# Loading V from ScalarE's hardware queue instead of SyncE's in a one-token attention kernel

## The chip, the core and the metric

The kernel runs on one core of a Trainium2 chip. The metric is the device time of one execution in microseconds (us). Before the change the median of three runs is 1298.89 us (1298.85 to 1299.34).

The core has five instruction streams: TensorE (PE, with its weight loads as PEld), VectorE (DVE), ScalarE (ACT), GpSimd (POOL) and SyncE (SP). All transfers between main memory and on-chip memory are moved by the core's 16 DMA engines, whichever stream issues them. A stream issues its own instructions in order; streams wait for one another only on semaphores.

## The reference, cut to what matters

```python
def _A_ref(x, k_cache, v_cache, wq, wo):        # x: (2, 1, 512); caches: (2, 32, 8192, 128), float32
    B, Sq, D = x.shape
    H, Dh = 32, 128
    q = (x @ wq).reshape(B, Sq, H, Dh).transpose(0, 2, 1, 3)
    scores = jnp.einsum("bhqd,bhkd->bhqk", q, k_cache) * (Dh ** -0.5)
    p = _softmax(scores, axis=-1)
    o = jnp.einsum("bhqk,bhkd->bhqd", p, v_cache)
    return o.transpose(0, 2, 1, 3).reshape(B, Sq, H * Dh) @ wo
...
x = A_x
xn = _layernorm(x, axis=-1)
s = _A_ref(xn, A_k_cache, A_v_cache, A_wq, A_wo)
g = _silu(_B_ref(xn, B_w1, B_b1, B_w2, B_b2))   # a small MLP of each token
return x + s * g
```

Two tokens, 32 heads each, 8192 cached keys and values of 128 floats per head. The caches of K and V are 268 MB each, and every number of them is used once.

## The kernel before, in words

**Tiling.** The 64 (token, head) combinations are taken two at a time: `N = 32` pairs, numbered n = 0 to 31. K of a pair is 8 MB and is laid out on 128 partitions with 64 KB on each (a head has 64 partitions, a partition has 128 keys). V of a pair has the same layout. One load of K or V is thus one DMA of 128 rows of 64 KB, 8 rows for each of the 16 DMA engines.

**Buffers.** K has two buffers, `kb[0]` and `kb[1]`, used in turn. V has a single buffer, `vb`, which at the start also holds the weights of the small parts and at the end the matrix `wo`. V of the last pair goes to `kb[1]` instead.

**The work on a pair n.** VectorE multiplies K by the query in place in two halves (`scores_mul`, L559), adds up each key's products in two halves (`scores_sum`, L566) and takes the largest score (`max_rows`, L570). PE and VectorE turn this into the largest score of each head (`max_dve`, L573 and L576). ScalarE computes the exponentials into `PZ` (`exps`, L583 to L591). PE multiplies them with V in 32 matmuls (`weighted`, L610, 64 matmul records in the profile), ScalarE copies the result out of the accumulator (`O4`, L617), PE picks each head's part (L619) and VectorE stores it into `Z` (`spread`, L625).

**The order on VectorE.** The steps of two neighbouring pairs are interleaved by hand. In turn n VectorE runs: first half of the product for pair n, the head's maximum for pair n-1, second half of the product, both sums for pair n, the maximum, and `spread` of pair n-1. So `weighted(n-1)` needs the exponentials of pair n-1, which come after the first product of pair n; and the last step of VectorE's turn n needs `weighted(n-1)`.

**The order on SyncE's queue.** All loads are issued by SyncE, in program order: ..., V(n), K(n+2), V(n+1), K(n+3), ... V(n) waits until `weighted(n-1)` has read `vb`. K(n+2) waits until `scores_sum(n)` has read its buffer. At the end come V(31) in two halves, and `wo` in seven pieces, which wait until `weighted(30)` has read `vb`.

**Loops.** A planner (`Plan`) collects all operations, derives the semaphore waits from what each reads and writes, and puts the operations that repeat from pair to pair into a hardware loop of its own on each engine. SyncE has no loop: its loads are written out one by one. ScalarE's loop runs over turns 1 to 31 and holds `exps` and the copy of `O4`.

Of the kernel before, what the change touches and what calls it, by code (L numbers as in the profile page):

```python
# [21 lines left out]
class Plan:  # L22
# [18 lines left out]
    def op(self, eng, fn, r=(), w=(), over=(), it=None, loop=False, dma=None):  # L41


        o = Op()
        o.eng, o.fn, o.it, o.loop, o.dma, o.tell = eng, fn, it, loop, dma, False
        need = {}

        def after(d, war):
            if d.dma is None and dma is None and d.eng == eng and (eng == "pe" or war):
                return  # L50
            if d.dma is None:
                if need.get(d.eng) is None or need[d.eng].idx < d.idx:
                    need[d.eng] = d
            else:
                k = ("dma", d.dma)
                if need.get(k) is None or need[k].idx < d.idx:
                    need[k] = d

        for k in r:
            if k in self.writer:  # L60
                after(self.writer[k], False)
        for k in list(w) + list(over):
            if k in self.writer:
                after(self.writer[k], False)
            for d in self.readers.get(k, ()):
                after(d, True)
        clock = self.clock[eng]
        need = {k: d for k, d in need.items() if clock.get(k, 0) < d.idx}
        o.deps = [(k, d) for k, d in need.items()
                  if not any(e is not d and e.done.get(k, 0) >= d.idx for e in need.values())]  # L70
        for _, d in o.deps:
            for k, v in d.done.items():
                clock[k] = max(clock.get(k, 0), v)
        own = eng if dma is None else ("dma", dma)
        self.count[own] = o.idx = self.count.get(own, 0) + 1
        o.done = dict(clock)
        o.done[own] = o.idx
        for k in w:
            self.writer[k] = o
            self.readers[k] = []  # L80
        for k in r:
            if k not in w:
                self.readers.setdefault(k, []).append(o)
        self.ops.append(o)
# [80 lines left out]
def decode_kernel(nc, x, kc, vc, wq, wo, w1, b1, w2, b2, out):  # L165
    P = 128
    B, H, S, DH = kc.shape
# [3 lines left out]
    U = 2  # L171
    HP = P // U
    KP = S // HP
    HH = H // U
    N = B * HH
# [25 lines left out]
    op = plan.op  # L201

    def pe(fn, r=(), w=(), it=None, loop=False):
        op("pe", fn, r, w, it=it, loop=loop)
# [4 lines left out]
    def act(fn, r=(), w=(), it=None, loop=False):  # L209
        op("act", fn, r, w, it=it, loop=loop)  # L210
# [4 lines left out]
    def sbuf(name, shape):  # L215
        return nc.alloc_sbuf_tensor(name, shape, F32).ap()

    def psum(name, shape):
        return nc.alloc_psum_tensor(name, shape, F32).ap()
# [5 lines left out]
    vb = sbuf("vb", [P, KP * DH])  # L225
    kbuf = [t.rearrange("p (j d) -> p j d", d=DH) for t in kb]
    vbuf = vb.rearrange("p (j d) -> p j d", d=DH)
# [19 lines left out]
    half = sbuf("half", [P, UP])  # L247
# [6 lines left out]
    ZR = sbuf("ZR", [P, B * P])  # L254

    PZ = sbuf("PZ", [P, NT, U, JW])
# [4 lines left out]
    BIAS = sbuf("bias", [P, U])  # L261
    RS = sbuf("rs", [P, 1])
    O4 = sbuf("o4", [P, JW * DH])
# [9 lines left out]
    boot = []  # L273

    def take(name, p, n, base=0, at=None):

        if at is None:
            at = used[0]
            used[0] += n
            assert used[0] <= KP * DH  # L280
        boot.append(name)
        return vb[base:base + p, at:at + n]
# [22 lines left out]
    h = take("h", P, WR * B).rearrange("p (r b) -> p r b", b=B)  # L305
# [5 lines left out]
    PO = psum("po", [P, JW * DH])  # L311
# [6 lines left out]
    def bank():  # L318
        i = turn[0] % 4
        turn[0] += 1  # L320
        return scratch[i], f"s{i}"
# [3 lines left out]
    vf = vc.rearrange("b h s d -> (b h s d)").rearrange("(n p j d) -> n p j d", p=P, j=KP, d=DH)  # L325
    M = KP // 2

    def load(dst, src, sem, w, over=()):
        op("sp", lambda: nc.sync.dma_start(dst, src), (), w, over=over, dma=sem)  # L329

    def load_k(n):
        i = (n + 1) % 2
        if n in (0, N - 1):
            for s in range(2):
                load(kbuf[i][:, s * M:(s + 1) * M], kf[n][:, s * M:(s + 1) * M], f"k{i}{s}", [("kb", i, s)])
            return
        load(kbuf[i], kf[n], f"kb{i}", [("kb", i, s) for s in range(2)])
# [186 lines left out]
    for k in range(N // NB):  # L524

        b, e = divmod(k, HH // NB)
        i, g = divmod(e, GQ)
        p, kp = bank()
# [9 lines left out]
    PT, PM, PN = (t for t in scratch[:3])  # L538
    load_k(1)

    def load_v(n):
        load(vbuf, vf[n], "v", ["vb"], over=boot)

    def cols(t, a, n):

        return t[:, a:a + n] if isinstance(a, int) else t[:, bass.ds(a, n)]
# [32 lines left out]

    def exps(n):  # L580
        one = dict(it=n + 1, loop=n < N - 1)
        pe(lambda i: matmul(PN[:, :U], srow, NM, start=True, stop=True), ["srow", "nm"], ["s2"], **one)  # L582
        act(lambda i: nc.scalar.copy(BIAS, PN[:, :U]), ["s2"], ["bias"], **one)  # L583
        sc = SC.rearrange("p (t j) -> p t j", j=JW)
        for s in range(U):
            r = slice(HP * s, HP * (s + 1))
            act(lambda i, r=r, s=s: nc.scalar.activation(PZ[r, :, s, :], sc[r], AF.Exp, bias=BIAS[r, s:s + 1],  # L587
                                                         scale=SCALE, accum_out=RS[r]),
                ["bias", ("sc", 0), ("sc", 1)], [("PZ", s), ("rs", s)], **one)

        act(lambda i: nc.scalar.activation(cols(ZR, i * UP - UP, UP), half, AF.Copy, scale=RS),  # L591
            ["half"] + [("rs", s) for s in range(U)], [("ZR", n)], **one)

    def busy(n):

        for _ in range(n):
            pe(lambda: matmul(scratch[3], ident, Q[:, :512], start=True, stop=True),
               ["ident"] + [("Q", k) for k in range(512 // (NB * DH))], ["s3"])

    def weighted(n):  # L600

        one = dict(it=n + 1, loop=n < N - 1)
        last = n == N - 1
        v = kbuf[1] if last else vbuf
        for t in range(NT):
            j = t % QT
            keys = [("kb", 1, t * JW // M)] if last else ["vb"]
            pe(lambda i, t=t, j=j, v=v: matmul(PO[R * j:R * j + U * JW, :], PZ[:, t].rearrange("p s j -> p (s j)"),  # L610
                                               v[:, t * JW:(t + 1) * JW, :].rearrange("p j d -> p (j d)"),
                                               start=(t < QT), stop=(t + QT >= NT)),
               keys + [("PZ", s) for s in range(U)], ["po"], **one)
        if last:
            busy(1)

        act(lambda i: nc.scalar.copy(O4, PO), ["po"], ["o4"], **one)  # L617
        for k in range(JW):
            pe(lambda i, k=k: matmul(PT[:, :U], O4[:, k * DH:(k + 1) * DH], mod[:, k:U * JW:JW],  # L619
                                     start=(k == 0), stop=(k == JW - 1)), ["o4", "mod"], ["s0"], **one)  # L620
# [9 lines left out]
    for n in range(N):  # L630
        scores_mul(n, 0)
        if n:
            max_dve(n - 1)
            exps(n - 1)
        scores_mul(n, 1)
        if n == 0:
            gates()
            load_v(0)

        if n:  # L640
            weighted(n - 1)
            if n < N - 1:
                load_v(n)
        scores_sum(n, 0)
        scores_sum(n, 1)
        max_rows(n)
        if n:
            spread(n - 1)

        if n + 2 < N:  # L650
            load_k(n + 2)
        elif n + 2 == N:
            for s in range(2):
                load(kbuf[1][:, s * M:(s + 1) * M], vf[N - 1][:, s * M:(s + 1) * M], f"v1{s}", [("kb", 1, s)])
# [7 lines left out]

    max_dve(N - 1)
    exps(N - 1)
    weighted(N - 1)
    spread(N - 1)

# [91 lines left out]
```

## Time and profile before

| | |
|---|---|
| median of three runs | 1298.89 us |
| profiled execution, its own time | 1298.97 us |
| its span (first to last instruction) | 1297.7 us |
| bytes read from main memory | 559.30 MB |
| mean rate over the span | 431 GB/s |
| ScalarE busy | 78.0 us (6%) |
| PE busy | 411.7 us (32%) |

The profile of one execution is read in several views. One lists the engines' busy time; one lists the DMA queues with packets, megabytes and the share of the 16 DMA engines' time that their packets took; one (the chain of waits) follows the last instruction back, at each step to what released it; one lists groups of equal instructions with count, total busy time and mean nanoseconds of one; the timeline lists instructions in order: start, duration, engine, line, operation, output<-input, count, and in brackets how long the engine stood idle before it and what released it. "SPq" is the issuing of a DMA by SyncE. "Windows" gives busy time in a chosen stretch.

### The profile page before, as it was taken

The page shows a single profiled execution, that of the slowest core. Times are in us where ns is not written, and L with a number is a line of the kernel's source. Part 1 is how long each engine was busy: PE and PEld are TensorE (multiplying, and loading weights), DVE is VectorE, ACT ScalarE, POOL GpSimd, SP SyncE. Part 2 cuts the span into 40 slices and gives each one's busy share as a digit, 9 for nine tenths or more (in the row PEclk, how much of TensorE's full clock was granted, in tenths as well). Part 3 has the DMA queues.
Part 4 walks back from the last instruction along what each step waited for, and adds up shares of the span by engine and source line. Part 5 has one row for each costly group of instructions (what it writes and reads, how often), then busy time and mean ns, then how long its engine had stood idle before and what let it go on. Part 6 is the DMA issues. An engine that isn't in the chain of part 4 may idle for free.

```text
span 1297.7 us, 6944 instructions
## 1 busy us (share of the span) xinstructions
PE 411.7 (32%) x2796; PEld 123.9 (10%) x2796; DVE 1138.0 (88%) x294; ACT 78.0 (6%) x250; POOL 1.4 (0%) x8
## 2 busy tenths in 40 slices
PE   5602333312333312333311333321333321333327
PEld 1100011000101000101100101000001100001103
DVE  3699999888889988889988889988888988888991
ACT  1200000000000000000000000000000000000000
POOL 0000000000000000000000000000000000000000
PEclk9856666556666556666555666655666655666659
DMA  9999999999999999999999999999999999999998
GB/s 400 449 425 440 428 428 442 426 442 426 434 438 424 446 424 440 430 426 444 426 438 430 428 442 426 442 426 432 440 424 446 424 440 430 424 446 426 427 430 373
DMA packets 11231, 559.42 MB, mean 431 GB/s; under 512 B 1364, under 2 KB 1620, under 8 KB 1880
## 3 DMA queue, kind: packets, MB, share of 16 engines
q1 hardware_dynamic: 11224, 559.33, 99.7%
q8 instruction: 4, 0.07, 0.0%
q14 instruction: 3, 0.02, 0.0%
HBM read 559.30 MB, written 0.03 MB: 431 GB/s over the span
## 4 chain that ended last, share of the span: by engine, by line
DMA 72%; PE 23%; DVE 3%; issue 1%; ACT 0%; SPq 0%; another core or an unknown queue 0%; DVEq 0%; ACTq 0%
DMA vb<-in_A_v_cache_dram 67%; PE po L610 22%; DMA kb<-in_A_wq_dram 3%; DMA vb<-in_A_wo_dram 2%; DVE kb L559 1%; DVE sc L566 1%; PE po L518 1%; SPq L329 0%; PE acc L703 0%; PE s L531 0%; PE wide L711 0%; ACT PZ L587 0%; DVE gate L503 0%; PE s L582 0%; ACT Q L533 0%
## 5 line engine op out<-in xcount | busy, mean ns | idle before, releaser
L559 DVE TENSOR_TENSOR kb<-kb,Q 128x8192 f32<-128x8192 f32 x64 | 555.6, 8682 | 107.9 <-DMA kb<-in_A_k_cache_dram 96.7
L566 DVE TENSOR_REDUCE sc<-kb 128x64 f32<-128x8192 f32 x64 | 552.3, 8666 | 0.0
L610 PE MATMUL po<-vb,PZ 128*8 128x512 f32 x1984 | 288.8, 748 | 293.7 <-DMA vb<-in_A_v_cache_dram 292.0
L582 PE MATMUL s<-nm,srow 1*128 1x2 f32 x64 | 18.4, 355 | 364.1 <-DVE nm L576 364.1
L610 PEld LDWEIGHTS po<-vb,PZ 128*8 128x8 f32 x1984 | 57.5, 104 | 499.0 <-issue 497.2
L573 PE MATMUL s<-ident,mx 128*1 128x128 f32 x32 | 11.8, 369 | 180.2 <-DVE mx L570 180.2
L582 PEld LDWEIGHTS s<-nm,srow 1*128 1x128 f32 x64 | 15.7, 302 | 373.3 <-DVE nm L576 373.3
L617 ACT COPY o<-po 128x512 f32<-128x512 f32 x32 | 18.8, 586 | 541.7 <-PE po L610 541.7
L583 ACT COPY bias<-s 128x2 f32<-128x2 f32 x32 | 5.1, 160 | 609.3 <-PE s L582 609.3
L619 PE MATMUL s<-mod,o 128*128 128x2 f32 x256 | 33.6, 253 | 22.1 <-ACT o L617 22.1
L619 PEld LDWEIGHTS s<-mod,o 128*128 128x128 f32 x256 | 31.1, 191 | 51.3 <-ACT o L617 51.3
L587 ACT ACTIVATE PZ<-sc,bias 64x128 f32<-64x128 f32 x64 | 25.5, 399 | 1.8
L573 PEld LDWEIGHTS s<-ident,mx 128*1 128x1 f32 x32 | 2.5, 79 | 183.0 <-DVE mx L570 183.0
L625 DVE TENSOR_TENSOR Z<-blk,s 128x8 f32 (+1 forms) x32 | 5.2, 163 | 12.4 <-PE s L619 12.4
L443 DVE COPY vb<-vb 2x384 f32<-2x384 f32 x4 | 1.8, 500 | 14.7 <-ACT vb L439 14.7
L587 ACT ACTIVATION_READ_ACCUMULATOR PZ<-sc,bias 64x1 f32 x64 | 11.8, 185 | 0.0
L435 PE MATMUL s<-vb 128*2 128x512 f32 (+1 forms) x24 | 11.3, 620 | 0.3 <-ACT vb L393 0.3
L570 DVE TENSOR_REDUCE mx<-sc 128x1 f32<-128x128 f32 x32 | 9.1, 286 | 1.1
L591 ACT ACTIVATE ZR<-half,rs 128x8 f32 (+1 forms) x32 | 9.6, 301 | 4.1
L518 PE MATMUL po<-kb,vb 128*4 128x512 f32 x64 | 8.4, 684 | 2.6 <-DMA kb<-in_A_wq_dram 2.6
L610 PE MATMUL po<-kb,PZ 128*8 128x512 f32 x64 | 8.8, 709 | 1.4 <-ACT PZ L587 1.4
L576 DVE TENSOR_REDUCE nm<-s 1x2 f32<-1x128 f32 x32 | 8.7, 272 | 0.3 <-PE s L573 0.3
(101 smaller groups left out, 80.7 us busy)
## 6 DMA issues: line engine op xcount, KB each, us to landing
kb<-in_A_k_cache_dram SPq DMA_DIRECT2D x4, 4096.0 KB, 43.3
kb<-in_A_v_cache_dram SPq DMA_DIRECT2D x2, 4096.0 KB, 40.4
vb<-in_B_w_dram SPq DMA_DIRECT2D x2, 2752.0 KB, 12.3
vb<-in_A_wo_dram SPq DMA_DIRECT2D x1, 4096.0 KB, 19.8
vb<-in_A_wo_dram SPq DMA_DIRECT2D x1, 2048.0 KB, 24.3
vb<-in_A_wo_dram SPq DMA_DIRECT2D x1, 1280.0 KB, 26.9
vb<-in_A_wo_dram SPq DMA_DIRECT2D x2, 256.0 KB, 27.0
vb<-in_A_v_cache_dram SPq DMA_DIRECT2D x31, 29.2
```

What stands on the lines that cost most here:

```text
L435: pe(lambda f=f, w=w, ph=ph, c=c: matmul(ph[:B, :w], yT[:, c, :], w1_sb[:, c, f:f + w], start=(c == 0), stop=False), ["yT", "w1"], [k])
L518: pe(lambda i=i, c=c, wv=wv, a=a, j=j, hd=hd: matmul(PO[R * j:R * j + NQ * B, :].rearrange("m (h d) -> m h d", d=DH), xnT[:, c, a:a + NQ * ...
L559: vector(n, n, lambda n: nc.vector.tensor_tensor(out=k, in0=k, in1=cols(Q, n * DH, DH).unsqueeze(1).to_broadcast([P, M, DH]), op=ALU.mult) ...
L566: vector(n, n, lambda n: nc.vector.tensor_reduce(out=SC[:, s * M:(s + 1) * M], in_=k, axis=AX.X, op=ALU.add), [("kb", i, s)], [("sc", s)])
L570: vector(n, n, lambda n: nc.vector.tensor_reduce(out=MX, in_=SC, axis=AX.X, op=ALU.max), [("sc", 0), ("sc", 1)], ["mx"])
L573: pe(lambda i: transpose(PM[:1, :P], MX, ident), ["mx", "ident"], ["s1"], it=n, loop=n > 0)
L582: pe(lambda i: matmul(PN[:, :U], srow, NM, start=True, stop=True), ["srow", "nm"], ["s2"], **one)
L587: act(lambda i, r=r, s=s: nc.scalar.activation(PZ[r, :, s, :], sc[r], AF.Exp, bias=BIAS[r, s:s + 1], scale=SCALE, accum_out=RS[r]), ["bias ...
L591: act(lambda i: nc.scalar.activation(cols(ZR, i * UP - UP, UP), half, AF.Copy, scale=RS), ["half"] + [("rs", s) for s in range(U)], [("ZR" ...
L610: pe(lambda i, t=t, j=j, v=v: matmul(PO[R * j:R * j + U * JW, :], PZ[:, t].rearrange("p s j -> p (s j)"), v[:, t * JW:(t + 1) * JW, :].rea ...
L617: act(lambda i: nc.scalar.copy(O4, PO), ["po"], ["o4"], **one)
L619: pe(lambda i, k=k: matmul(PT[:, :U], O4[:, k * DH:(k + 1) * DH], mod[:, k:U * JW:JW], start=(k == 0), stop=(k == JW - 1)), ["o4", "mod"], ...
```

## The change

V of pairs 1 to 30 is issued by ScalarE inside its loop, right behind the copy of `O4`. V(0) stays with SyncE, as does V(31). The buffers, the arithmetic and the waits for the buffers stay as they were. For the address of V(n) the loop's register is used. ScalarE's loop runs over turns 1 to 30 instead of 1 to 31; the last turn is written out behind it (`two`, and the copy of `O4`, with `loop=n < N - 2`).

```diff
+    vrows = vc.rearrange("b h s d -> (b h s d)").rearrange("(n p e) -> n p e", p=P, e=KP * DH)
+
     def load_v(n):
-        load(vbuf, vf[n], "v", ["vb"], over=boot)
+        if n == 0:
+            load(vbuf, vf[0], "v", ["vb"], over=boot)
+            return
+        op("act", lambda i: nc.scalar.dma_start(
+            vb, vrows[i if isinstance(i, int) else bass.ds(i, 1)].rearrange("p e -> p e" if isinstance(i, int) else "o p e -> (o p) e")),
+            (), ["vb"], it=n, loop=n < N - 1, dma="v")
...
     def exps(n):
         one = dict(it=n + 1, loop=n < N - 1)
+        two = dict(it=n + 1, loop=n < N - 2)
...
-        act(lambda i: nc.scalar.copy(O4, PO), ["po"], ["o4"], **one)
+        act(lambda i: nc.scalar.copy(O4, PO), ["po"], ["o4"], it=n + 1, loop=n < N - 2)
```

SyncE's queue at the first pairs, before (`kb0`, `kb1` and `vb` are the buffers; each row is one DMA):

```order
L329 DMA kb1<-in_A_k_cache_dram 128x8192 x2
L329 DMA kb0<-in_A_k_cache_dram 128x16384
L329 DMA vb<-in_A_v_cache_dram 128x16384
L329 DMA kb1<-in_A_k_cache_dram 128x16384
L329 DMA vb<-in_A_v_cache_dram 128x16384
L329 DMA kb0<-in_A_k_cache_dram 128x16384
L329 DMA vb<-in_A_v_cache_dram 128x16384
```

The same place, with the change:

```order
L329 DMA kb1<-in_A_k_cache_dram 128x8192 x2
L329 DMA kb0<-in_A_k_cache_dram 128x16384
L329 DMA vb<-in_A_v_cache_dram 128x16384
L329 DMA kb1<-in_A_k_cache_dram 128x16384
L329 DMA kb0<-in_A_k_cache_dram 128x16384
L329 DMA kb1<-in_A_k_cache_dram 128x16384
```

The 30 rows of V between the rows of K are gone; a load of K now follows the load of K before it, and no load of V stands between.

ScalarE's loop before, from its first row to the branch back:

```order
L583 COPY bias<-s 128x2
L107 ISA
L587 ACTIVATE PZ,rs<-sc,bias 64x32x4 x2
L107 REGISTER_ALU
L591 ISA
L591 ACTIVATE ZR<-half,rs 128x8
L107 REGISTER_ALU
L617 COPY o<-po 128x512
L158 REGISTER_ALU
L158 COMPARE_AND_BRANCH
```

The same loop with the change (line numbers are 8 higher in the new file):

```order
L591 COPY bias<-s 128x2
L107 ISA
L595 ACTIVATE PZ,rs<-sc,bias 64x32x4 x2
L107 REGISTER_ALU
L599 ISA
L599 ACTIVATE ZR<-half,rs 128x8
L107 REGISTER_ALU
L625 COPY o<-po 128x512
L547 ISA
L547 DMA vb<-in_A_v_cache_dram 128x16384
L158 REGISTER_ALU
L158 COMPARE_AND_BRANCH
```

The load stands at the end of the turn, behind the copy that already waits for the last matmul on `vb`.

More of the change, by code (lines that the diff above doesn't have):

```diff
@@ L581, in exps @@
         one = dict(it=n + 1, loop=n < N - 1)
+        two = dict(it=n + 1, loop=n < N - 2)
         pe(lambda i: matmul(PN[:, :U], srow, NM, start=True, stop=True), ["srow", "nm"], ["s2"], **one)
-        act(lambda i: nc.scalar.copy(BIAS, PN[:, :U]), ["s2"], ["bias"], **one)
+        act(lambda i: nc.scalar.copy(BIAS, PN[:, :U]), ["s2"], ["bias"], **two)
         sc = SC.rearrange("p (t j) -> p t j", j=JW)
@@ L588, in exps @@
                                                          scale=SCALE, accum_out=RS[r]),
-                ["bias", ("sc", 0), ("sc", 1)], [("PZ", s), ("rs", s)], **one)
+                ["bias", ("sc", 0), ("sc", 1)], [("PZ", s), ("rs", s)], **two)
         act(lambda i: nc.scalar.activation(cols(ZR, i * UP - UP, UP), half, AF.Copy, scale=RS),
-            ["half"] + [("rs", s) for s in range(U)], [("ZR", n)], **one)
+            ["half"] + [("rs", s) for s in range(U)], [("ZR", n)], **two)
     def busy(n):
```

## The prediction

> **What bounds the kernel now.** I read the page's busy times, its table of DMA queues and its chain of waits first.
>
> ```profile
> span 1297.7 us, 6944 instructions
> PE 411.7 (32%) x2796; PEld 123.9 (10%) x2796; DVE 1138.0 (88%) x294; ACT 78.0 (6%) x250; POOL 1.4 (0%) x8
> ...
> q1 hardware_dynamic: 11224, 559.33, 99.7%
> ...
> DMA 72%; PE 23%; DVE 3%; issue 1%; ACT 0%; SPq 0%; another core or an unknown queue 0%; DVEq 0%; ACTq 0%
> ```
>
> One queue, q1, keeps the 16 DMA engines at work 99.7% of the span. VectorE, at 88%, is the next limit. The profiled execution took 1298.97 us, 0.08 above the median of the runs, so I work against it directly. Next the timeline of one pair in the middle, cut to the rows that hand over, and a window from one `weighted` to the next:
>
> ```profile
> 607.37 0.33 SPq L329 DMA_DIRECT2D vb<-in_A_v_cache_dram  x1
> 607.38 0.59 ACT L617 COPY o<-po 128x512 f32<-128x512 f32 x1 [16.98 <-PE po L610]
> ...
> 608.02 1.05 PE L619 MATMUL s<-mod,o 128*128 128x2 f32 x8 [0.71 <-ACT o L617]
> 613.90 0.33 SPq L329 DMA_DIRECT2D kb<-in_A_k_cache_dram  x1
> ...
> 614.12 0.16 DVE L625 TENSOR_TENSOR Z<-blk,s 128x8 f32 x1
> ...
> 617.92 8.69 DVE L559 TENSOR_TENSOR kb<-kb,Q 128x8192 f32<-128x8192 f32 x1 [3.64 <-DMA kb<-in_A_k_cache_dram]
> ...
> 637.23 9.90 PE L610 MATMUL po<-vb,PZ 128*8 128x512 f32 x64 [9.79 <-DMA vb<-in_A_v_cache_dram]
> ...
> 652.62 0.33 SPq L329 DMA_DIRECT2D kb<-in_A_k_cache_dram  x1
> ...
> 656.61 8.69 DVE L559 TENSOR_TENSOR kb<-kb,Q 128x8192 f32<-128x8192 f32 x1 [3.59 <-DMA kb<-in_A_k_cache_dram]
> ```
>
> ```profile
> core 0: us, PE busy (x) PEld busy (x) DVE busy (x) ACT busy (x) POOL busy (x), PEclk, DMA share, GB/s
> 637.23:675.94 38.71, 11.90 (x76) 3.48 (x77) 35.09 (x8) 2.03 (x7) 0.00 (x0) 0.59 1.00 433
> ```
>
> A pair takes 656.61 - 617.92 = 38.7 us, two loads of 19.35 us with no gap (DMA share 1.00, 433 GB/s). The loads run strictly one after the other: K is there at 617.92, V at 637.23, the next K at 656.61. The V that was issued at 607.37 waits in the queue for the K ahead of it. That wait is free: while it lasts the engines move K. VectorE stands 3.6 us a pair, waiting for K. So nothing can be gained but the missing 0.3% of DMA time, 4 us. The question is whether the engines keep their gapless work when V and K come from two queues.
>
> **The change part by part.** Removed: 30 issues of V on SyncE's queue. Added: the same 30 issues at the end of ScalarE's turn.
>
> ```profile
> SPq L329 <- PE po L610: 978.0, 31, 33.0
> SPq L329 <- DVE mx L570: 209.0, 31, 17.3
> ```
>
> SyncE stood 978 us behind V's wait for `weighted`. But it was always past it before K's buffer came free: V goes out at 607.37, and SyncE then waits until VectorE's last sum ends at 613.90 and issues K at once. So K's issue gains nothing from a queue of its own. An issue costs 0.33 us; on ScalarE (busy 6%) it hides in that engine's idle time, since ScalarE next has to wait for the matmul of L582. V's issue comes behind the copy, up to 0.6 us later than before. Turn 31, now written out, holds the same instructions: nothing.
>
> What changes is the order of the bytes. V(n) no longer stands behind K(n+1) but beside it. Does an engine serve a second queue in the middle of a load? The run has one instance that can be looked at, in the first V load (its issue in the timeline, its time to landing in the DMA view of the stretch 40 to 80 us):
>
> ```profile
> 66.35 0.33 SPq L329 DMA_DIRECT2D vb<-in_A_v_cache_dram  x1
> ...
> vb<-in_A_v_cache_dram SPq DMA_DIRECT2D x1, 28.9
> ```
>
> It landed at 95.25, so its own 19.35 us began near 75.9. The DMA view of the stretch 86 to 92 us lies within them:
>
> ```profile
> DMA packets 40, 2.57 MB, mean 429 GB/s; under 512 B 0, under 2 KB 0, under 8 KB 0
> ...
> q1 hardware_dynamic: 39, 2.56, 98.9%
> q8 instruction: 1, 0.02, 1.1%
> ```
>
> q1 moves rows of 64 KB (2.56 MB by 39), and none of the small packets that close a load is among them. Yet a packet of q8 gets through. So an engine turns to another queue between two rows of a load. I take it that K and V, both queued, get a row each in turn, half the rate each.
>
> The Trainium skill, page "DMA: Bandwidth & Descriptors", section "Queues, rings and completion order", says that an engine takes turns between queues, but only at the end of a packet, typically 9 to 17 descriptors. An engine's 8 rows and its closing write would be one such packet, loads would go whole, and the sum would be 0 where the row of q8 gives some 130 us. The trace speaks against the long packet; it shows it for an instruction queue, not for two load queues.
>
> Now one pair under equal sharing, as a period T. Let w be the end of `weighted(n-1)`, when V(n) may be issued. VectorE's `spread` follows at w + 1.7 (607.37 to 609.07, the end of L619), takes 0.16, and the next turn to the end of its sums takes 652.62 - 617.92 = 34.7. If K is there in time, the next K is issued at w + 36.6. On V's side `weighted` takes 288.8 / 31 = 9.3 us, 9.4 with its start:
>
> ```profile
> L610 PE MATMUL po<-vb,PZ 128*8 128x512 f32 x1984 | 288.8, 748 | 293.7 <-DMA vb<-in_A_v_cache_dram 292.0
> ...
> out_dram<-res SPq DMA_DIRECT2D x1, 28.0 KB, 1.4
> ```
>
> So V(n) must have landed at w + T - 9.4. The start and landing of a load, which no row of the gapless loop shows, I bound from the last row: 28 KB take 1.4 us from issue to landing, and I use 1.4 for both ends together (nearest row; not below 0, and at most double under load).
>
> The walk: K goes out at w + 36.6 - T, so before w. It runs alone until V joins, about 7 us, and shares its other 12.3 us at half rate for 24.6. It lands near w + 26, well before VectorE needs it. V then has the engines alone and lands near w + 33.6. From there until the next K is issued **nothing is queued**: V's buffer is being read by PE, both K buffers are full, and VectorE, which has to free one, had stood at `spread` for `weighted(n-1)`. The idle stretch is b = (w + 36.6) - (w + T - 9.4) + 1.4 = 47.4 - T. The DMA work is still 38.7, so T = 38.7 + b, T = (38.7 + 47.4) / 2 = 43.05 and b = **4.35 us a pair**. In the old order, V first and then K, PE's reading of V was always covered by a K load that had waited behind it; that cover goes.
>
> Thirty pairs: 30 x 4.35 = 130.5. The beginning costs some more, as the chain's pieces show:
>
> ```profile
> 104.93 29.07 DMA vb<-in_A_v_cache_dram
> 134.12 8.92 PE po L610 x64
> ```
>
> V(1) is issued at 104.9 and lands near 134; K(2) ahead of it is there 19.35 sooner, at 114.7. With sharing V(1) joins at about 106.5, when K(2) has 8 us left: these take 16, V(1) has 8 done, and its other 11.3 beside K(3) take 22.7. It lands near 145, `weighted` ends near 154.6, and this pair takes 49.7: 6 more than a later one. The end gives some back:
>
> ```profile
> 1265.76 3.44 SPq L329 DMA_DIRECT2D vb<-in_A_wo_dram  x7
> ...
> 1266.61 26.91 DMA vb<-in_A_wo_dram
> ```
>
> Today `wo` is issued while V(31) is still being moved, and 1297.7 - 1265.76 = 32 us pass from there to the end. With sharing V(31) has landed by then; `wo` alone needs 1.4 + 19.35, and 4.2 follow (1297.7 - 1293.5): 25, so -7. Sum: 130.5 + 6 - 7 = 129.5, and 1298.97 + 129.5 = **1428 us**.
>
> **Bounds of the sum.** Double the 1.4: b + 0.7, +21. The two queues together move 3% less (no row shows two; 433 GB/s is the only rate seen): +0.55 a pair, +17. Or 3% more: -17. `weighted` ran between 8.7 and 10.05 us in the chain's pieces with PE's granted clock; if more idle time gives it a higher clock, 8.7, then -0.35 a pair, -10:
>
> ```profile
> 1179.06 8.70 PE po L610 x64
> ...
> 172.82 10.05 PE po L610 x64
> ```
>
> Together about 1395 to 1470 for this case.
>
> **The rivals.** *Whole loads, in order of issue* (not slower): if an engine finishes all 8 rows of a load before it turns to the other queue, V(n), issued at 607.37, goes behind the running K and ahead of the K issued at 613.90, just as now. It decides whenever V is issued before K, and that lead is 6.5 us now. The time is 1299 us, at best 4 less, since only 0.3% is idle. That is what the packet rule of the Trainium skill, told above, comes to. For it: nothing here shows two load queues; against it: the q8 packet. The same time results if the new queue's rows are strung into q1. Chance 0.11, with 0.02 of it for a gain over 0.2%.
>
> *V is served first, or gets more than half.* With V always first, K's rows wait for the rest of one V load (7 us), then start, and are broken off by the whole next one: 7 + 19.35 + 19.35 + 1 = 46.7 from issue to landing. VectorE needs it 35.5 after the issue and waits 11; the next K lands in time. Two pairs take 2 x 35.1 + 11 = 81.2, a pair 40.6, 1.9 more than now: 30 x 1.9 = 57, **1356 us**. Nothing in the rows speaks for an order among queues. Chance 0.10.
>
> *K gets more than half.* K lands earlier, which helps nobody, and V still lands when all bytes are moved: T is the same, the first pair is longer by up to 10, 1438. It lies within the forecast's bounds. Chance 0.05.
>
> **How the numbers follow.** Equal sharing 0.74, V favoured 0.10, K favoured 0.05, whole loads 0.11. The predicted time is that of equal sharing, 1428. The range from 1345 to 1470 takes in the first three cases and leaves out whole loads and some of the size errors, near 0.2. A change under 0.2% (2.6 us) can't be told from none: faster 0.02, same 0.09, slower 0.89.
>
> **What would show it.** Two hardware queues, each with about half of the loop's bytes. A mean rate near 390 GB/s (559 MB over 1427 us), and idle DMA stretches of 4 to 5 us a pair while PE is in `weighted`. V's time from issue to landing near 33 us instead of 29.2, K's near 33 instead of 42.5. VectorE no longer waits for K at L559 but for L619 at `spread`, some 8 us a pair (43 - 35.1). If K is still seen landing 19.35 us before V with a DMA share of 1.00, sharing is wrong; if VectorE waits 11 us for K in every second pair, V goes first.

## The result and the profile after

The changed kernel takes 1447.22 us in the median (1444.86 to 1450.07, four runs) beside 1298.87 before: a ratio of 1.1142, 95% interval 1.1122 to 1.1163. It is slower by 148 us. 1428 was predicted, with a range of 1345 to 1470.

The page of the changed kernel's profiled execution, which took 1450.07 us, the longest of the four: span, busy times, DMA packets, the queues, the chain that ended last, and the two rows of loads that changed most (count, median us from issue to landing):

```profile
span 1448.7 us, 6999 instructions
PE 403.7 (28%) x2796; PEld 121.8 (8%) x2796; DVE 1139.7 (79%) x294; ACT 78.0 (5%) x250; POOL 1.4 (0%) x8
...
DMA packets 11230, 559.41 MB, mean 386 GB/s; under 512 B 1364, under 2 KB 1620, under 8 KB 1880
...
q1 hardware_dynamic: 6904, 307.67, 50.4%
q10 hardware_dynamic: 4320, 251.66, 40.2%
...
DMA 73%; PE 22%; DVE 3%; issue 1%; ACT 0%; SPq 0%; ACTq 0%; DVEq 0%
...
kb<-in_A_k_cache_dram SPq DMA_DIRECT2D x30, 34.0
vb<-in_A_v_cache_dram ACTq DMA_DIRECT2D x30, 33.9
```

The same bytes are moved. ScalarE's loads run on a queue of their own, q10. The two queues keep the engines busy 90.6% of the span where one kept them busy 99.7%: 9.4% of 1448.7 is 136 us of idle engines, where there were 4. The other 19 of the 151 us between the two spans are packets that took longer: 90.6% of 1448.7 us is 1312.5 us of packet time, where 99.7% of 1297.7 was 1293.8 (more on them below, at the size of a pair). The work of the other engines is unchanged: VectorE is busy 1139.7 us, as before (1138.0), in a longer span. The chain's shares look alike, DMA 73% and PE 22%, which shows that shares don't tell where a difference of 11% came from.

The DMA view for 20 us in which both queues have a load:

```profile
DMA packets 128, 8.39 MB, mean 419 GB/s; under 512 B 0, under 2 KB 0, under 8 KB 0
...
q1 hardware_dynamic: 64, 4.19, 48.4%
q10 hardware_dynamic: 64, 4.19, 48.4%
```

64 rows of 64 KB each: exactly half and half. Half and half would also fit whole loads that change over in the middle of these 20 us. The rows that begin between 647.0 and 649.4 us and those that begin between 649.4 and 651.8 us, in each case one for every engine, show the turns themselves:

```profile
q10 hardware_dynamic: 16, 1.05, 100.8%
...
q1 hardware_dynamic: 16, 1.05, 100.9%
```

First all 16 engines move a row of V, then all 16 a row of K. The timeline of the pair around it, the issue of K from the timeline of SyncE's queue, and two windows (the last three numbers of a row are PE's granted clock, the DMA share and GB/s):

```profile
633.35 8.63 PE L618 MATMUL po<-vb,PZ 128*8 128x512 f32 x64 [24.60 <-DMA vb<-in_A_v_cache_dram]
...
642.06 0.59 ACT L625 COPY o<-po 128x512 f32<-128x512 f32 x1 [31.63 <-PE po L618]
642.20 0.34 ACTq L547 DMA_DIRECT2D vb<-in_A_v_cache_dram  x1
...
643.93 0.16 DVE L633 TENSOR_TENSOR Z<-blk,s 128x8 f32 x1 [9.71 <-PE s L580]
...
675.12 9.93 PE L618 MATMUL po<-vb,PZ 128*8 128x512 f32 x64 [21.51 <-DMA vb<-in_A_v_cache_dram]
```

```profile
678.78 0.33 SPq L329 DMA_DIRECT2D kb<-in_A_k_cache_dram  x1
```

```profile
676.00:679.00 3.00, 3.00 (x20) 0.58 (x16) 2.97 (x2) 0.00 (x0) 0.00 (x0) 0.50 0.00 0
642.06:685.12 43.06, 11.70 (x75) 3.41 (x75) 35.11 (x7) 2.03 (x7) 0.00 (x0) 0.60 0.86 365
```

V has landed when PE starts at 675.12. K(n+2) is issued only at 678.78, when VectorE's sums end, and in between the DMA share is 0.00: PE reads the one V buffer, both K buffers are full. The wait of VectorE has moved as well, from L559 (K) to L633 (`spread`), as the table of waits shows (total, times, longest):

```profile
DVE Z L633 <- PE s L580: 235.3, 29, 12.9
...
DVE kb L566 <- DMA kb<-in_A_k_cache_dram: 2.8, 1, 2.8
```

(The profile names L580 as releaser; `spread` needs L627, which PE issues right before it.) Before, VectorE waited 96.7 us for K in 28 pairs.

### The profile page after: what moved, and what is told of

Its sections match the earlier page's. It is cut to its first block, busy times and chain, and to the rows that moved or that the text cites. A ratio compares the mean times of both kernels' runs of the same rounds, so it can differ in the third digit from the quotient of the medians.

```text
span 1448.7 us, 6999 instructions
## 1 busy us (share of the span) xinstructions
PE 403.7 (28%) x2796; PEld 121.8 (8%) x2796; DVE 1139.7 (79%) x294; ACT 78.0 (5%) x250; POOL 1.4 (0%) x8
## 4 chain that ended last, share of the span: by engine, by line
DMA 73%; PE 22%; DVE 3%; issue 1%; ACT 0%; SPq 0%; ACTq 0%; DVEq 0%
DMA vb<-in_A_v_cache_dram 71%; PE po L618 21%; DMA kb<-in_A_wq_dram 2%; DVE kb L566 1%; DVE sc L573 1%; PE po L518 1%; PE wide L698 0%; PE s L605 0%; ACT o L625 0%; PE s L627 0%; ACT PZ L595 0%; SPq L329 0%; PE s L590 0%; PE s L531 0%; PE acc L711 0%
## 5 line engine op out<-in xcount | busy, mean ns | idle before, releaser
L633 DVE TENSOR_TENSOR Z<-blk,s 128x8 f32 (+1 forms) x32 | 5.2, 163 | 253.2 <-PE s L580 235.3
L627 PE MATMUL s<-mod,o 128*128 128x2 f32 x256 | 33.6, 253 | 22.1 <-ACT o L625 22.1
L627 PEld LDWEIGHTS s<-mod,o 128*128 128x128 f32 x256 | 31.0, 191 | 51.3 <-ACT o L625 51.3
L580 PE MATMUL s<-ident,mx 128*1 128x128 f32 x32 | 8.8, 276 | 37.9 <-DVE mx L577 37.9
L531 PE MATMUL s<-o,ident 128*64 128x512 f32 x32 | 7.1, 595 | 0.7 <-ACT o L523 0.7
```

Source lines behind the costliest of these rows:

```text
L580: pe(lambda i: transpose(PM[:1, :P], MX, ident), ["mx", "ident"], ["s1"], it=n, loop=n > 0)
```

## The experiments

The theory: the engines take a row from each queue in turn; V therefore lands late, and while PE reads V nothing is queued. The main rival: it costs to issue from ScalarE (its place behind the copy, the loop, the address from a register). Each kernel was timed beside the kernel of before on the same chip.

**One queue again, but ScalarE's.** All loads from K(2) on are issued by ScalarE, in the old order.

```diff
     def act(fn, r=(), w=(), it=None, loop=False):
-        op("act", fn, r, w, it=it, loop=loop)
+        op("act", fn, r, w, it=it)
...
     def load(dst, src, sem, w, over=()):
-        op("sp", lambda: nc.sync.dma_start(dst, src), (), w, over=over, dma=sem)
+        if late[0]:
+            op("act", lambda: nc.scalar.dma_start(dst, src), (), w, over=over, dma=sem)
+        else:
+            op("sp", lambda: nc.sync.dma_start(dst, src), (), w, over=over, dma=sem)
...
             load_v(0)
+            late[0] = True
```

> All loads from K(2) on, of K, of V and of wo, are issued by ScalarE in the old order, so that one queue holds both again; ScalarE's work is written out without its loop. Sharing theory (two queues get a row each in turn, and V's buffer is read while nothing is queued): one queue restores V before K, 38.7 us a pair, 1299 us, within 4. Rival (issuing on ScalarE, behind its copies, is what costs): it has twice the issues of the changed kernel, so 1447 us or more.

Measured: 1301.53 us, ratio 1.0021 (1.0011 to 1.0031). Its queues:

```profile
q10 hardware_dynamic: 10080, 520.10, 92.7%
q1 hardware_dynamic: 1144, 39.23, 7.0%
```

70 issues on ScalarE instead of 30, the DMA engines 99.7% busy, and the loss is gone but for 2.8 us (1298.69 before, beside it). Issuing from ScalarE isn't what costs; the loss comes with the second queue.

**V on ScalarE, without loop or register.**

```diff
-        op("act", fn, r, w, it=it, loop=loop)
+        op("act", fn, r, w, it=it)
...
-            (), ["vb"], it=n, loop=n < N - 1, dma="v")
+            (), ["vb"], it=n, dma="v")
```

> The changed kernel with ScalarE's work written out: no loop, fixed addresses instead of the register's. Sharing theory: nothing changes, 1447 us within 10. Rival (the loop's branch or the address from a register delays V's issue): below 1430 us, towards 1299.

Measured: 1447.02 us, ratio 1.1133 (1.1114 to 1.1152). The loop and the register play no part.

**A wait more: K(n+2) behind V(n).** A dependence on the landing of V is added to K's issue, without making K a reader of V's buffer.

```diff
...
-        load(kbuf[i], kf[n], f"kb{i}", [("kb", i, s) for s in range(2)])
+        load(kbuf[i], kf[n], f"kb{i}", [("kb", i, s) for s in range(2)], behind=["vb"] if n > 2 else ())
```

(The two halves of K(31) get the same wait.)

> The changed kernel with one wait more: K(n+2) is issued only when V(n) has landed. Sharing theory: V(n) then shares only with what is left of K(n+1); K is always under way while PE reads V's buffer, and the engines idle only from V's landing to K's first row, about 2.2 us a pair: 40.9 us a pair, 1366 us (1345 to 1385), faster than the changed kernel by some 80 us although a wait was added. Rival (two queues cost by themselves, or ScalarE's issue does): a wait more can't help, 1447 us or more.

Measured: 1379.36 us, ratio 1.0617 (1.0599 to 1.0635): 68 us faster than the changed kernel, by adding a wait. Two pieces of its chain, two pairs apart:

```profile
627.89 31.42 DMA kb<-in_A_k_cache_dram
...
710.07 31.48 DMA kb<-in_A_k_cache_dram
```

(710.07 - 627.89) / 2 = 41.1 us a pair, 2.4 above the DMA work of 38.7: the idle stretch is now only the landing of V and the start of K. So this also measures the two ends of a load that the trace of before could not show.

**V in halves.** The first half of V(n+1) is issued when PE has read the first half of V(n).

```diff
+    def load_v_half(n, g):
+        c = slice(g * M * DH, (g + 1) * M * DH)
+        op("act", lambda i: nc.scalar.dma_start(
+            vb[:, c], (vrows[i] if isinstance(i, int) else vrows[bass.ds(i, 1)].rearrange("o p e -> (o p) e"))[:, c]),
+            (), [("vb", g)], it=n, loop=n < N - 1, dma=f"v{g}")
...
+            if t == NT // 2 - 1 and n < N - 2:
+                load_v_half(n + 1, 0)
...
-                load_v(n)
+                load_v_half(n, 1)
```

> The changed kernel with V loaded in two halves of 4 MB, each with its own wait: the first half of V(n+1) is issued as soon as PE has read the first half of V(n); wo's first piece waits for the first half of the buffer likewise. Sharing theory: V's queue is no longer empty while PE reads, the idle stretch closes nearly or wholly: 1299 to 1330 us by a walk through the rows; 1380 us if it only gets shorter by half of weighted. Rival (issuing on ScalarE costs): 60 issues instead of 30, more than 1447 us.

Measured: 1313.77 us, ratio 1.0115 (1.0098 to 1.0132). Still two queues and 60 issues from ScalarE, and nine tenths of the loss are gone:

```profile
q1 hardware_dynamic: 7048, 307.67, 54.3%
q10 hardware_dynamic: 8640, 251.66, 44.5%
```

98.8% busy. A window of 1000 us in the middle shows no loss at all:

```profile
250.00:1250.00 1000.00, 343.54 (x1948) 88.44 (x1940) 903.36 (x181) 51.41 (x177) 0.00 (x0) 0.63 1.00 432
```

DMA share 1.00 and 432 GB/s, against 433 in the window of the kernel before: sharing by itself costs nothing that shows once something is always queued. The 15 us that remain lie at the end: the last fortieth of the span has 197 GB/s where the kernel before has 373. The loss takes both, sharing and a single buffer that is released all at once.

**A dose on PE.** Five matmuls that nobody reads, before the last matmul that reads V's buffer, in the changed kernel and in the one of before.

```diff
+            if t == NT - 1 and not last:
+                for _ in range(5):
+                    pe(lambda i: matmul(scratch[3], ident, Q[:, :512], start=True, stop=True),
+                       ["ident", ("Q", 0)], ["s3"], **one)
```

> The changed kernel with five idle matmuls (128x512, about 0.94 us each, so 4.7 us a pair) on PE before the last matmul that reads V's buffer, for pairs 0 to 30; their result is not used. Sharing theory: the pair is half of (DMA work 38.7 + the loop through spread, VectorE and weighted), so half of 4.7 is paid: +2.35 a pair, +70 us, 1517 us (1495 to 1535). Rival (V's loop alone sets the pair): the whole 4.7 is paid, +140 us, 1590. Rival (DMA alone sets it): no change, 1447.

Measured: 1524.0 us, ratio 1.1734 (1.1715 to 1.1754), 76.8 above the changed kernel. The timeline gives the dose, the chain the issues of V(1), V(4) and V(28):

```profile
666.90 4.56 PE L620 MATMUL s<-Q,ident 128*128 128x512 f32 x10
...
109.44 36.35 DMA vb<-in_A_v_cache_dram
...
252.80 35.81 DMA vb<-in_A_v_cache_dram
...
1365.43 30.26 DMA vb<-in_A_v_cache_dram
```

From V(4) to V(28), (1365.43 - 252.80) / 24 = 46.36 us a pair, 2.44 more than in the changed kernel (43.92, worked out below). That is 0.53 of the dose, close to the half that was expected; a pair is neither DMA's time nor V's loop alone, but near the mean of the two. The first dose counts nearly whole: V(1) goes out at 109.44 instead of 105.17, 4.3 us later.

> The kernel of before with the same five idle matmuls a pair. Sharing theory: a K load that stands in the one queue covers PE's reading of V, so 4.7 us more cost nothing: 1299 us, within 3. Rival (weighted is on the path that sets the end, as the chain of waits lists it with 22%): +140 us, 1440.

Measured: 1304.14 us (1301.97 to 1310.38), ratio 1.0046 (1.003 to 1.0062). So the same dose costs 5 us where K covers it. This is slightly outside the 3 that were expected. The span was 1305.5 us and q1's share in it:

```profile
q1 hardware_dynamic: 11224, 559.33, 99.5%
```

99.5% of 1305.5 is 1299 us of packets, against 1294 before: the engines weren't idle, the packets took longer. The single packets of the trace show where. 245 rows of 64 KB took more than 2.48 us, 2.81 on average, where 2.42 is usual. None of them began while the dose ran; the 879 rows that did took 2.42. Half of them began within 3 us of an issue of V. With the dose, K is mostly issued 0.4 to 1.4 us behind V, where 5.3 to 6.6 us lay between the two before. What makes these rows longer isn't shown.

**Roles exchanged.** K from ScalarE, V from SyncE, starting from the kernel of before.

```diff
...
-        load(kbuf[i], kf[n], f"kb{i}", [("kb", i, s) for s in range(2)])
+        load(kbuf[i], kf[n], f"kb{i}", [("kb", i, s) for s in range(2)], eng="act" if n > 1 else "sp")
```

> K(2) to K(31) and V(31) are issued by ScalarE (written out, no loop), V(0) to V(30) and wo by SyncE: the same two queues with the roles exchanged. Sharing theory: each queue gets a row in turn, whichever it is: 1447 us within 15. Rival (one of the two queues is served first): V on the other queue then gets the other treatment, and the time moves towards 1356 us (V first) or stays only if K was first before.

Measured: 1654.05 us, ratio 1.2738 (1.2717 to 1.2759). Neither the theory nor its rival had expected that. The timeline:

```profile
713.09 9.80 PE L611 MATMUL po<-vb,PZ 128*8 128x512 f32 x64 [29.36 <-DMA vb<-in_A_v_cache_dram]
...
722.96 0.59 ACT L618 COPY o<-po 128x512 f32<-128x512 f32 x1 [37.65 <-PE po L611]
722.97 0.35 ACTq L330 DMA_DIRECT2D kb<-in_A_k_cache_dram  x1
...
764.42 9.73 PE L611 MATMUL po<-vb,PZ 128*8 128x512 f32 x64 [29.91 <-DMA vb<-in_A_v_cache_dram]
...
774.23 0.35 ACTq L330 DMA_DIRECT2D kb<-in_A_k_cache_dram  x1
```

ScalarE works in order. K(n+2) could have gone out at the end of VectorE's sums, but it stands behind the copy that waits for `weighted(n-1)`. Both queues are then empty during all of `weighted`: 774.23 - 722.97 = 51.3 us a pair, that is 38.7 of DMA work, 9.9 from PE's start to the issue, and 2.7 for the two ends of a load. So this run said nothing about which queue is served first. The next one takes the copy out of K's way. The rest of its edit is that of the exchange.

```diff
...
+        scores_sum(n, 0)
+        scores_sum(n, 1)
+        if n + 2 < N:
+            load_k(n + 2)
         if n:
             weighted(n - 1)
             if n < N - 1:
                 load_v(n)
-        scores_sum(n, 0)
-        scores_sum(n, 1)
...
-        if n + 2 < N:
-            load_k(n + 2)
-        elif n + 2 == N:
+        if n + 2 == N:
```

> The kernel with the roles of the queues exchanged, but ScalarE now issues K(n+2) ahead of the copy that waits for weighted(n-1), so that K goes out when VectorE's sums end, as in the changed kernel. In the first exchange K went out only with V, at the end of weighted: nothing was queued while PE read V, 38.7 + 9.8 + the two ends of a load = about 51 us a pair. Sharing theory: with K's issue free of that, the same walk as for the changed kernel, 1447 us within 15. Rival (the second queue is served worse, so that K on it, or V, loses): still above 1550 us, or towards 1356 if V gains.

Measured: 1452.77 us, ratio 1.1182 (1.1163 to 1.1201). With the queues exchanged the time is that of the changed kernel within 6 us: neither queue is preferred.

## Why the prediction came out as it did

**What bounds the kernel, and that nothing can be gained:** right. No version ran below the kernel of before.

**Each load gets a row in turn:** right. All 16 engines move a row of V and then a row of K, 64 rows against 64 in 20 us, and the exchanged queues give nearly the same time. The whole-load rival, 1299 us, and the one with V first, 1356, both fall. What the Trainium skill says of taking turns at the end of a packet ("DMA: Bandwidth & Descriptors", "Queues, rings and completion order") holds here with a packet of one row of 64 KB, not of the 9 descriptors of a load.

**The idle stretch while PE reads V:** right in place and cause; the halves take it away, the dose makes it longer by half of itself. VectorE's wait moved to `spread` as forecast, 235.3 / 29 = 8.1 us a pair (some 8).

**The size of a pair:** 43.05 predicted; the mechanism held and one term of the sum was too small. The chain shows the issues of V:

```profile
105.17 40.70 DMA vb<-in_A_v_cache_dram
...
156.17 38.78 DMA vb<-in_A_v_cache_dram
...
204.60 31.47 DMA vb<-in_A_v_cache_dram
...
245.64 36.83 DMA vb<-in_A_v_cache_dram
...
1299.74 30.27 DMA vb<-in_A_v_cache_dram
1338.75 32.24 DMA vb<-in_A_v_cache_dram
1379.72 29.93 DMA vb<-in_A_v_cache_dram
```

From V(4) to V(28), (1299.74 - 245.64) / 24 = 43.92 us a pair. The term that was too small is the start and landing of a load: I took 1.4 us for both ends from the 28 KB output. The run with K behind V gives 2.4 and the first exchange 2.7. Part of it is the first row that each engine moves after standing idle. K is issued at 678.78; here are the 16 rows that begin between 679 and 682 us and the 16 that begin between 682 and 685:

```profile
q1 hardware_dynamic: 16, 1.05, 102.4%
...
q1 hardware_dynamic: 16, 1.05, 80.6%
```

102.4% of 3 us is 3.07 us for a first row, 80.6% is 2.42 for a second one. In 30 pairs that is 30 x 0.65 = 20 us, which accounts for the longer packet time of the page (19). With 2.7 the same formula gives (38.7 + 36.6 + 9.4 + 2.7) / 2 = 43.7. The other 0.2 come from two terms that were read a little short: from V's landing to the next issue of V these 24 pairs take 9.6 us on average (9.4 used), and from V's issue to K's they take 36.6 and 36.9 in turn (36.6 used). "At most double" had held the 2.7; the value was taken from a load too small to stand for one of 8 MB. 24 x 0.87 = 21 us.

**The beginning:** the first pair took 51.0 (49.7 predicted), but the second 48.4 and not 43: another 5. I had walked through the first one only. **The last three pairs,** from V(28) to `wo`, took less: 119.6 us (1299.74 to 1419.38) where I had 129, so -9.5. K(31) and V(31) are issued in two halves, the first as soon as VectorE's first sum has freed half of the buffer. K(31) starts at 1328.08, where a whole load would have gone out at 1299.74 + 36.6 = 1336.3. So the engines have work while PE reads V, which I had not walked through:

```profile
1330.00:1336.50 6.50, 6.37 (x48) 1.43 (x52) 6.50 (x1) 0.00 (x0) 0.00 (x0) 0.78 0.98 408
```

**The end:** from the issue of `wo` 29.3 us (1419.38 to 1448.7), not 25. I let `wo`'s landing set the end. The chain shows PE instead:

```profile
1409.77 9.59 PE po L618 x64
...
1423.50 9.50 PE po L618 x64
...
1435.76 2.66 PE s L605 x6
1438.42 5.31 PE wide L698 x48
```

V(31) had landed, as predicted, but its `weighted` stood behind that of pair 30, since V(30) came so late; PE's work one after the other ends last. +4.

Together 21 + 1 + 5 - 2 (the third pair, 41.0) - 9.5 + 4 = 20 us, which with 129.5 makes 150 of the 151 us between the two spans.

## What to carry to other kernels

A queue's order is part of the schedule. Where one queue keeps the DMA engines full, a transfer that waits in it costs nothing, and it covers the time in which the buffer of another is being read; giving it its own queue makes the two share the rate, so that the one that is waited for lands later (V 33.9 us after its issue instead of 29.2), and then leaves the engines with nothing. Before splitting loads over two queues, ask what is queued at the moment the last one lands; and if a load is moved to a compute engine, ask behind which wait it will stand there, since that cost more here (51.3 us a pair) than the sharing (43.9).

## What was not expected of the hardware

Start and landing of an 8 MB load took 2.4 to 2.7 us together in these runs, against 1.4 for 28 KB including its transfer; 0.65 of that is the first row of each engine, 3.07 us instead of 2.42. And with the dose in the kernel of before the same packets took 0.4% more DMA time, 1299 instead of 1294 us. PE was busier there (44% instead of 32%), but no row that began while the dose ran was slow; the slow ones begin after it, and most of them shortly behind the issues of V and K, which there follow each other closely. The cause wasn't tried.
